# The last pair's fold and the mixing's first sums: one step or three

## The chip, the cores and the metric

The kernel runs on one core of a Trainium2 chip. The metric is the device time of one execution in microseconds (us). The kernel before has a median of 1599.43 us over three runs (1600.13, 1599.43 and 1596.14). One more execution was recorded by the hardware profiler; that one is what the profile below shows.

## The reference

For each of 8 batches and 8 heads (sequence length 576, head size 64), attention keeps only scores within `tau` of the row's maximum. The heads' outputs are joined to rows of 512, and those go through a Fourier mixing, a layer norm and a two-layer channel network:

```python
scores = np.matmul(q, k.transpose(0, 1, 3, 2)) / np.sqrt(64)
thresh = np.max(scores, axis=-1, keepdims=True) - tau
attn = softmax(np.where(scores >= thresh, scores, -1e9))
x = np.matmul(attn, v).transpose(0, 2, 1, 3).reshape(8, 576, 512)

mixed = np.real(np.fft.fft(np.fft.fft(x, axis=1), axis=2))
u = x + mixed
un = (u - mean(u)) / np.sqrt(var(u) + 1e-6)
out = u + np.maximum(un @ w_ch1, 0.0) @ w_ch2      # 512 -> 2048 -> 512
```

All of it is in 32-bit floats.

## The kernel before, in words

**Tiling.** The sequence of 576 rows is cut into 5 query tiles (4 of 128 rows, one of 64). Two heads are handled as a pair, so that a batch has 4 pairs x 5 tiles = 20 steps. A step `i` belongs to pair `n` and tile `t`; below, m is the step's number inside its batch, m = `i % 20`. Batches 2 to 7 run in the late loop (L1692 and after), 120 steps. Everything of the two stages is interleaved there: while the attention of batch b runs, the rows of earlier batches go through mixing and channel network.

**One step of the late loop.** It is written out by hand, in this order:

1. `scores(i)`: TensorE (PE) makes the scores of both heads (L427; L433 for the short tile).
2. At t = 3 and t = 1 the values' product `pv` (L627) for a finished half of a pair, whose result ScalarE (ACT) copies out (L634, `x_first`).
3. `softmax_first`: VectorE (DVE) makes the negated row maxima `neg` (L506, two instructions), ACT the exponentials `e` (L512) and the thresholds `thr` (L516).
4. At m = 2: the rest of `last_fold`, then `start_batch`, which makes the mixing of the batch before available and plans the channel work.
5. `fill(True)`: filler matmuls of the channel network for PE. DVE and ACT jobs that these bring along are held back until after step 6.
6. `softmax_second`: DVE cuts `e` at the threshold and sums it (L527), adds a small number to the sum `den` (L531) and inverts it (L534). Then the held jobs.
7. One part of the mixing, if one is open. At t = 1 the fold of the previous pair begins.
8. The transposes of the weights of step i-1: a small one `pe` (L578), then two groups `pw` (L596), with a `fill()` between them.
9. `softmax_third`: ACT scales `e` by 1/`den` (L540). At t = 3 `prep_pair` transposes the next pair's keys and queries on DVE (L398, L399, L401).
10. `factors()` of a row group whose statistics are ready, then a last `fill()`, which also takes one part of the mixing.
11. DMA issues on SyncE (SP): `load_v` at t = 2, `load_pair` at t = 4.

**What orders the work.** Each engine takes its instructions in the order in which this loop issues them. PE's filler is metered by a budget: `per_slot` is the work still to do, less a reserve `keep`, divided by the number of fills in a batch. A unit of 2048 stands for one block of four 128x512 matmuls. With `keep` the loop leaves 3 x 7 such blocks over for later. `ps.tile(..., tag="mm", bufs=4)` are four banks of PSUM that `pw`, `pv`, `py`, `po` and others share: a new use of a bank waits until the old content was read.

**The fold of a batch's last pair** (`fold_rows`, L660 to L698) is on DVE; for the other pairs it is on GpSimd (POOL). It takes the pair's output `x` and makes two `half` rows (L678, sum and difference with the mirrored row), four pieces of `f` from them (L683), and two small ones for the edges (L690, L694). At m = 1 both `half` instructions and all four pieces are issued, at m = 2 the small ones.

**The mixing** (`mixing`, L719 and after) is a generator. It first forms sums and differences over channel chunks, `fold_chunks` (L709 sums, L710 differences, 128x608 each), then the even and odd parts of `f` (L735, L731 twice, L731 for two more, L740; 128x304 each). After that the matmuls `py` (L750) read `f`, ACT copies them to `y_e` and `y_o` (L755, L760), `pa` (L767, L771) follow, and POOL adds the residual (L792). In the kernel before all of L709, L710, L735, L731 and L740 are issued at m = 2, and the first `py` at m = 3 just ahead of that step's `pe` and `pw`.

**Rows** (`Rows`, L824 and after) holds a group of 512 output rows. `load` turns them around through PSUM (`pn`, L836), ACT copies them to `u` (L842), DVE takes mean and variance (L844, L845). `factors` makes the inverse deviation: ACT takes the square root (L852), loads the table of the exponential again (L855), and DVE inverts the root (L856). `add` (L863) uses the result.

There are six places where a batch ends inside the late loop (m = 1 to 3 of steps 40, 60, 80, 100, 120 and 140 and after) and one after the loop, at the end of batch 7. I call the six *transitions* and the last one the *tail*.

Of the kernel before, what the change touches and what calls it, by code (L numbers as in the profile page):

```python
# [47 lines left out]
def kernel(  # L48
# [12 lines left out]
    nc = tc.nc  # L61
    B, H, S, D = q.shape
    DM = H * D
# [5 lines left out]
    NJ = HID // 128  # L69
# [7 lines left out]
    BT = 512  # L77
# [13 lines left out]
    FW = 304  # L91
# [297 lines left out]
            )  # L389

    def prep_pair(n):

        q_raw, k_raw = loaded.pop(n)
        kT = sb.tile([128, D + S], FP32, tag="kT", name="kT")
        nc.vector.transpose(kT[:, D : D + S], k_raw[:, :])  # L398
        nc.vector.transpose(kT[64:128, 0:D], k_raw[64:128, 512:S])  # L399
        qT = sb.tile([128, S], FP32, tag="qT", bufs=1, name="qT")  # L400
        nc.vector.transpose(qT[:, :], q_raw[:, :])  # L401
        heads[n] = (qT, kT, v_in[n % 2])
        if n + 1 < B * NPAIR and not late:
            load_pair(n + 1)
# [255 lines left out]
    def fold_rows(n):  # L660
        b, p = n // NPAIR, PAIRS[n % NPAIR]
        if late and n % NPAIR == 0:
            assert not mixes
            x = sb.tile([128, S], FP32, tag=f"x{p}", bufs=1, name=f"x{p}")
            nc.gpsimd.tensor_copy(x[:, :], xs[b][p][:, :])
            xs[b][p] = x
            swap_rows(n)
            yield
        x = xs[b][p]

        half = sb.tile([128, 2, HALF], FP32, tag="half", bufs=1, name="half")
        up, down = x[:, 1:HALF], _reversed(x[:, HALF + 1 : S])
        mid = S // 4

        last = n % NPAIR == NPAIR - 1
        eng = nc.vector if last else nc.gpsimd
        for c, op in enumerate((ALU.add, ALU.subtract)):
            eng.tensor_tensor(out=half[:, c, 1:HALF], in0=up, in1=down, op=op)  # L678
        yield
        for c, c0, op in (  # L680
            (0, 0, ALU.add), (0, 161, ALU.subtract), (1, FW, ALU.subtract), (1, FW + 161, ALU.add)
        ):
            eng.tensor_tensor(  # L683
                out=f[:, p, c0 : c0 + mid - 1], in0=half[:, c, 1:mid],
                in1=_reversed(half[:, c, mid + 1 : HALF]), op=op,
            )
            if late and last and c0 > 0 and c0 != FW:
                yield

        eng.tensor_tensor(  # L690
            out=f[:, p, mid - 1 : mid + 1], in0=_stepped(x, mid, -mid, 2),
            in1=_stepped(x, 3 * mid, -mid, 2), op=ALU.add,
        )
        eng.tensor_tensor(  # L694
            out=_stepped(f[:, p, :], 160, FW, 2), in0=_stepped(x, 0, mid, 2),
            in1=_stepped(x, HALF, mid, 2), op=ALU.subtract,
        )
        yield  # L698


        if n % NPAIR == 1 and b != 1:
            fold_halves(b)
# [3 lines left out]
        fold_chunks(nc.gpsimd, b, 1)  # L706

    def fold_chunks(eng, b, c):
        eng.tensor_tensor(out=sums[b][:, c, :], in0=f[:, c, :], in1=f[:, c + 2, :], op=ALU.add)  # L709
        eng.tensor_tensor(  # L710
            out=f[:, c + 2, :], in0=f[:, c, :], in1=f[:, c + 2, :], op=ALU.subtract
        )
# [6 lines left out]
    def mixing(b):  # L719
# [3 lines left out]


        E, O = slice(0, FW), slice(FW, 2 * FW)
        fold_chunks(nc.vector, b, 0)
        yield 0
        s01 = sums.pop(b)

# [94 lines left out]
    class Rows:  # L824
# [26 lines left out]
        def factors(self):  # L851
            nc.scalar.activation(  # L852
                out=self.rstd[:, :], in_=self.mv[:, :, 1], func=ACT.Sqrt, bias=eps[:, :], scale=1.0
            )
            nc.scalar.activation(out=warm[:, :], in_=eps[:, :], func=ACT.Exp)  # L855
            nc.vector.reciprocal(self.rstd[:, :], self.rstd[:, :])  # L856

        def add(self, t, cols, product):

            u = self.us[t][:, cols]  # L860
            if len(product.shape) == 3:
                u = u.rearrange("p (j n) -> p j n", j=2)
            nc.vector.scalar_tensor_tensor(  # L863
                out=u, in0=product, scalar=self.rstd[:, t : t + 1], in1=u,
                op0=ALU.mult, op1=ALU.add,
            )
# [574 lines left out]
    late = []  # L1441
    ended = []


    mixes = []
# [3 lines left out]
    per_batch = NPAIR * NT  # L1449
# [1 line left out]
    holding = []  # L1451
    held = []

    def fill(hold=False):
        nonlocal budget, spent
        holding[:] = [True] if hold else []
        budget += per_slot
        if mixes and not ended and not hold:
            mix(1)
        while work and spent < budget and work[0][0] < mixed:  # L1460
            done = next(work[0][1], None)
            if done is None:
                work.pop(0)
            else:
                spent += done
        holding.clear()
        if mixes and ended:
            mix(1)
# [123 lines left out]
    def start_batch(b):  # L1592

        nonlocal groups, todo, per_slot, budget
        mixes.append(mixing(b))
        todo += MIX
        while groups < NG and BT * (groups + 1) <= (b + 1) * S:
            rows = Rows(groups)
            work.append((b, channels(rows) if groups == 0 else two_level(groups, rows), rows))
            todo += cost(groups)  # L1600
            groups += 1

        keep = 4 * BT * NJ * DM // 128 if b == 0 else 3 * 7 * 2048
        per_slot = (todo - spent - keep) / (3 * per_batch)
        budget = spent

    def mix(count):
        nonlocal spent, mixed
        for _ in range(count):
            done = next(mixes[0], None)  # L1610
            if done is None:
                mixes.pop(0)
                mixed += 1
                break
            spent += done
# [72 lines left out]
        fold_more()  # L1688

    late.append(True)  # L1690

    for i in range(2 * per_batch, total):  # L1692


        n, t = divmod(i, NT)
# [11 lines left out]
            softmax_first(i)  # L1707
        next(values, None)
        if i % per_batch == 2:
            for _ in last_fold:  # L1710
                pass
            start_batch(i // per_batch - 1)
        fill(True)
        if i < total:
            softmax_second(i)
        while held:
            held.pop(0)()
        if mixes:
            mix(1)
        if t == 1:  # L1720
            if n % NPAIR:
                folds.append(fold_rows(n - 1))
            else:
                last_fold = fold_rows(n - 1)
                next(last_fold)
# [8 lines left out]
        if i < total:  # L1734
            softmax_third(i)
            if t == 1:
                prep_ends(n)
            if t == 2 and n + 1 < B * NPAIR:
                scale_q(n + 1)
            if t == 3 and n + 1 < B * NPAIR:  # L1740
                prep_pair(n + 1)
        if wanted:
            wanted.pop().factors()
        if i % per_batch == 1:
            next(last_fold)
        fill()
        if t == 2 and n + 1 < B * NPAIR:
            load_v(n + 1)
        if t == 4 and n + 2 < B * NPAIR:
# [21 lines left out]
    last_fold = fold_rows(B * NPAIR - 1)  # L1771
# [66 lines left out]
```

## Time and profile before

| what | value |
|---|---|
| median of three runs | 1599.43 us |
| the profiled execution, whole | 1599.32 us |
| its span, first to last instruction | 1596.8 us |
| PE busy | 1538.9 us (96% of the span) |
| DVE / ACT / POOL busy | 1097.3 / 908.5 / 805.1 us |
| mean granted PE clock | 0.989 of full speed |
| `half` L678 on DVE, shortest / median | 439 / 1372 ns |
| 1/rstd L856 on DVE, median | 177 ns, 9 times |

The profiled execution is 0.1 us under the median, and 2.5 us of its time lie outside the span. In the answers of the trace a line gives the start in us, the time in us, the engine, the line of the kernel, the operation, what it writes and reads (out<-in), the shape, and how many instructions stand in the group. In square brackets stands how long the engine stood idle before it, and what ended that. In tables by window, the share of time busy of each engine is followed by the number of its instructions, and after them come the granted PE clock (1.00 is full), the share of the DMA engines' time and their rate.

### The profile page before, as it was taken

To read this page: it belongs to the slowest core of one execution; us is meant where nothing else is said; L and a number is where in the kernel's file an instruction comes from. 1 tells how busy PE (TensorE), PEld (TensorE's weight loads), DVE (VectorE), ACT (ScalarE), POOL (GpSimd) and SP (SyncE) were. 2 spreads that over 40 slices of the span, in tenths; PEclk is the share of its full clock that TensorE was granted. 3 is DMA by queue.
4 is the path that set the end of the run, shared out by engine and by line. 5 is a ranking of instruction groups with operands and counts; after the bars stand their busy time and mean duration, and the time that the engine had idled before them with its cause. 6 is when DMAs were issued, how large, how long until landed. Compare 5 with 4: busy or idle time off the path is not lost.

```text
span 1596.8 us, 27063 instructions
## 1 busy us (share of the span) xinstructions
PE 1538.9 (96%) x9786; PEld 1191.1 (75%) x9786; DVE 1097.3 (69%) x2148; ACT 908.5 (57%) x1873; POOL 805.1 (50%) x1009
## 2 busy tenths in 40 slices
PE   8999989999999999989999999999999999999999
PEld 4555445555788877877787878877787778889999
DVE  6997886855869566775668567756577666655546
ACT  5775665554665566656666576656666666222231
POOL 6784665034445552546254633545264625546735
PEclk9999999999999999999999999999999999999999
DMA  6423221556956254634455345635464434546655
GB/s 156 134 58 115 75 76 36 161 154 201 301 171 205 77 158 127 201 112 142 133 159 160 119 129 151 184 101 155 128 181 127 135 124 150 200 150 226 242 192 186
DMA packets 248906, 239.30 MB, mean 150 GB/s; under 512 B 197027, under 2 KB 218533, under 8 KB 228678
## 3 DMA queue, kind: packets, MB, share of 16 engines
q1 hardware_dynamic: 246262, 237.28, 49.9%
q8 instruction: 78, 1.28, 0.3%
q10 hardware_dynamic: 2512, 0.30, 0.2%
q14 instruction: 54, 0.44, 0.1%
HBM read 205.93 MB, written 31.46 MB: 149 GB/s over the span
## 4 chain that ended last, share of the span: by engine, by line
PE 77%; DVE 14%; ACT 4%; issue 2%; POOL 2%; DMA 2%; SPq 0%; DVEq 0%; ACTq 0%; POOLq 0%
PE ph L1178 24%; PE po L1365 17%; PE pv L627 8%; PE sc L427 7%; PE pw L596 6%; PE po L901 4%; PE ph L877 2%; DVE e L467 2%; PE py L750 2%; PE sc L433 1%; PE pa L767 1%; DVE neg L451 1%; PE pe L578 1%; PE pa L771 1%; PE po L1344 1%
## 5 line engine op out<-in xcount | busy, mean ns | idle before, releaser
L512 ACT ACTIVATE e<-sc,neg 128x576 f32<-128x576 f32 x216 | 158.6, 734 | 139.2 <-DVE neg L506 138.8
L506 DVE TENSOR_REDUCE neg<-sc 128x1 f32<-128x576 f32 x216 | 154.0, 750 | 110.7 <-PE sc L427 103.1
L1365 PE MATMUL po<-w,w_all 128*128 128x128 f32 x1728 | 220.9, 278 | 0.8 <-ACT ends L584 0.8
L1365 PEld LDWEIGHTS po<-w,w_all 128*128 128x128 f32 x1728 | 206.9, 193 | 10.2 <-issue 5.5
L1115 DVE TENSOR_TENSOR hs<-ph,hs 128x512 f32<-128x512 f32 (+1 forms) x128 | 105.2, 822 | 157.8 <-PE ph L1178 101.7
L1124 POOL TENSOR_TENSOR w<-hs 128x512 f32<-128x512 f32 x32 | 42.1, 1318 | 317.4 <-ACT hs L1120 243.6
L596 PE MATMUL pw<-ident,e 128*128 128x128 f32 x1152 | 172.9, 277 | 17.9 <-ACT x_first L634 9.0
L1178 PE MATMUL ph<-u_t,w 128*128 128x256 f32 x768 | 180.5, 381 | 0.7 <-DMA w<-f 0.4
L527 DVE SCALAR_TENSOR_TENSOR e<-sc,thr,e 128x576 f32<-128x576 f32 x216 | 168.2, 812 | 17.7 <-ACT thr L516 17.5
L427 PE MATMUL sc<-kT,qT 64*128 64x288 f32 x1024 | 171.3, 434 | 9.1 <-DVE e L467 8.0
L598 ACT COPY e_t<-pw 128x512 f32<-128x512 f32 x256 | 148.7, 594 | 46.7 <-PE pw L596 45.5
L540 ACT ACTIVATE e<-e,den 128x576 f32<-128x576 f32 x216 | 157.6, 775 | 17.3 <-DVE den L534 16.4
L596 PEld LDWEIGHTS pw<-ident,e 128*128 128x128 f32 x1152 | 136.7, 142 | 36.3 <-ACT x_first L634 10.1
L1178 PEld LDWEIGHTS ph<-u_t,w 128*128 128x128 f32 x768 | 141.2, 190 | 23.5 <-issue 4.4
L1178 PE MATMUL ph<-w_all,w 128*128 128x256 f32 x672 | 157.1, 382 | 1.1 <-DVE w_all L1100 1.0
L427 PEld LDWEIGHTS sc<-kT,qT 64*128 64x128 f32 x1024 | 94.5, 188 | 64.2 <-issue 33.9
L1178 PEld LDWEIGHTS ph<-w_all,w 128*128 128x128 f32 x672 | 123.4, 190 | 23.9 <-issue 4.9
L1120 ACT ACTIVATE hs<-hs 128x512 f32<-128x512 f32 (+1 forms) x96 | 74.1, 771 | 114.1 <-DVE hs L1115 113.0
L1230 POOL TENSOR_TENSOR w_all<-w_all 128x128 f32<-128x128 f32 (+2 forms) x160 | 117.8, 753 | 29.9 <-DVE w_all L1385 22.4
L1365 PE MATMUL po<-w,hs 128*128 128x128 f32 x912 | 120.2, 279 | 0.0
L1365 PEld LDWEIGHTS po<-w,hs 128*128 128x128 f32 x912 | 110.5, 193 | 9.4 <-issue 7.2
L792 POOL TENSOR_TENSOR u_t<-x,tmp 128x289 f32<-128x289 f32 (+1 forms) x45 | 34.5, 766 | 104.8 <-DVE tmp L787 104.8
(225 smaller groups left out, 2996.7 us busy)
## 6 DMA issues: line engine op xcount, KB each, us to landing
w<-f SPq DMA_DIRECT2D x150, 1024.0 KB, 4.9
hs<-in_moe_w_ch_dram SPq DMA_DIRECT2D x23, 512.0 KB, 4.4
q_in<-in_q_dram SPq DMA_DIRECT2D x128, 72.0 KB, 3.3
out_dram<-u SPq DMA_DIRECT2D x36, 256.0 KB, 2.3
k_in<-in_k_dram SPq DMA_DIRECT2D x124, 72.0 KB, 3.1
v_in<-in_v_dram SPq DMA_DIRECT2D x64, 128.0 KB, 5.0
f<-w SPq DMA_DIRECT2D x14, 512.0 KB, 4.0
f<-w SPq DMA_DIRECT2D x7, 1024.0 KB, 4.8
```

The source lines that it names most:

```text
L427: nc.tensor.matmul(sc[j][:, c, 0:HALF], qT[hp, 128 * t : 128 * t + 128], kT[hp, k0 + HALF * c : k0 + HALF * (c + 1)], start=True, stop=True,)
L506: nc.vector.tensor_reduce(out=neg[:, j : j + 1], in_=sc[j][:, :, 0:HALF], axis=AXIS_XY, op=ALU.max, negate=True,)
L512: nc.scalar.activation(out=ej, in_=sc[j][:, :, 0:HALF], func=ACT.Exp, bias=neg[:, j : j + 1], scale=1.0)
L527: nc.vector.scalar_tensor_tensor(out=ej, in0=sc[j][:, :, 0:HALF], scalar=thr[:, j : j + 1], in1=ej, op0=ALU.is_ge, op1=ALU.mult, accum_out ...
L540: nc.scalar.activation(out=e[:, S * j : S * (j + 1)], in_=e[:, S * j : S * (j + 1)], func=ACT.Copy, scale=den[:, j : j + 1],)
L596: nc.tensor.transpose(pw[:, c, :], e[:, c0 : c0 + 128], ident[:, :])
L598: nc.scalar.copy(e_t[:, 4 * j : 4 * j + 4, qs], pw[:, :, :])
L627: nc.tensor.matmul(pv[64 * j : 64 * j + 64, 0:m], vt[:, 2 * c + j, :], e_t[:, 4 * j + c, 0:m] if c < 4 else ends[:, 0, 0:m], start=(c == 0 ...
L1115: nc.vector.tensor_tensor(out=to, in0=bank, in1=to if other is None else other, op=ALU.add)
L1178: nc.tensor.matmul(bank[:, 256 * q : 256 * q + 256].rearrange("p (two n) -> p two n", two=2), left[:, 256 * c + 128 * q : 256 * c + 128 * ...
L1230: return lambda: eng.tensor_tensor(out=to, in0=to, in1=other, op=ALU.add)
L1365: nc.tensor.matmul(to, lefts[m][j][:, s], right_[:, 128 * s : 128 * (s + 1)], start=jn in (0, 4) and s == 0, stop=s == 3, skip_group_check ...
```

## The change

- **The fold of the last pair**, for batches that end inside the loop (`apart`): the second `half` instruction goes to the last part of m = 1, after the step's second filler. Two pieces of `f` are issued in m = 2 before `softmax_second`, the other two and the small ones in m = 2 after it, in the place of that step's mixing part.
- **The mixing's first sums**: `chunks_in_parts` yields between L709 and L710. The last filler of m = 2 takes no part of the mixing. A new `mix(1)` stands in m = 3 ahead of `softmax_second`.
- **The pair's preparation**: `pair_in_parts` makes the transposed keys at t = 3 and the transposed queries at t = 4, in every pair of the late loop.
- **The inverse deviation** is made in the first `add` instead of in `factors`.
- **The reserve** `keep` of the late loop is 24 blocks instead of 21.

The number of instructions of each kind is the same.

```diff
@@ -389,14 +389,16 @@
             )
 
     def prep_pair(n):
+        for _ in pair_in_parts(n):
+            pass
+
+    def pair_in_parts(n):
 
         q_raw, k_raw = loaded.pop(n)
         kT = sb.tile([128, D + S], FP32, tag="kT", name="kT")
         nc.vector.transpose(kT[:, D : D + S], k_raw[:, :])
         nc.vector.transpose(kT[64:128, 0:D], k_raw[64:128, 512:S])
+        yield
         qT = sb.tile([128, S], FP32, tag="qT", bufs=1, name="qT")
         nc.vector.transpose(qT[:, :], q_raw[:, :])
         heads[n] = (qT, kT, v_in[n % 2])
@@ -674,8 +676,11 @@
 
         last = n % NPAIR == NPAIR - 1
         eng = nc.vector if last else nc.gpsimd
+        apart = late and last and b < B - 1
         for c, op in enumerate((ALU.add, ALU.subtract)):
             eng.tensor_tensor(out=half[:, c, 1:HALF], in0=up, in1=down, op=op)
+            if apart and c == 0:
+                yield
         yield
         for c, c0, op in (
             (0, 0, ALU.add), (0, 161, ALU.subtract), (1, FW, ALU.subtract), (1, FW + 161, ALU.add)
@@ -684,7 +689,7 @@
                 out=f[:, p, c0 : c0 + mid - 1], in0=half[:, c, 1:mid],
                 in1=_reversed(half[:, c, mid + 1 : HALF]), op=op,
             )
-            if late and last and c0 > 0 and c0 != FW:
+            if late and last and (c0 == 161 or c0 > FW and not apart):
                 yield
 
         eng.tensor_tensor(
@@ -706,7 +711,12 @@
         fold_chunks(nc.gpsimd, b, 1)
 
     def fold_chunks(eng, b, c):
+        for _ in chunks_in_parts(eng, b, c):
+            pass
+
+    def chunks_in_parts(eng, b, c):
         eng.tensor_tensor(out=sums[b][:, c, :], in0=f[:, c, :], in1=f[:, c + 2, :], op=ALU.add)
+        yield 0
         eng.tensor_tensor(
             out=f[:, c + 2, :], in0=f[:, c, :], in1=f[:, c + 2, :], op=ALU.subtract
         )
@@ -723,7 +733,11 @@
 
 
         E, O = slice(0, FW), slice(FW, 2 * FW)
-        fold_chunks(nc.vector, b, 0)
+        apart = late and b < B - 1
+        if apart:
+            yield from chunks_in_parts(nc.vector, b, 0)
+        else:
+            fold_chunks(nc.vector, b, 0)
         yield 0
         s01 = sums.pop(b)
 
@@ -853,10 +867,13 @@
                 out=self.rstd[:, :], in_=self.mv[:, :, 1], func=ACT.Sqrt, bias=eps[:, :], scale=1.0
             )
             nc.scalar.activation(out=warm[:, :], in_=eps[:, :], func=ACT.Exp)
-            nc.vector.reciprocal(self.rstd[:, :], self.rstd[:, :])
+            self.inverted = False
 
         def add(self, t, cols, product):
 
+            if not self.inverted:
+                nc.vector.reciprocal(self.rstd[:, :], self.rstd[:, :])
+                self.inverted = True
             u = self.us[t][:, cols]
             if len(product.shape) == 3:
                 u = u.rearrange("p (j n) -> p j n", j=2)
@@ -1451,11 +1468,11 @@
     holding = []
     held = []
 
-    def fill(hold=False):
+    def fill(hold=False, apart=False):
         nonlocal budget, spent
         holding[:] = [True] if hold else []
         budget += per_slot
-        if mixes and not ended and not hold:
+        if mixes and not ended and not hold and not apart:
             mix(1)
         while work and spent < budget and work[0][0] < mixed:
             done = next(work[0][1], None)
@@ -1600,7 +1617,7 @@
             todo += cost(groups)
             groups += 1
 
-        keep = 4 * BT * NJ * DM // 128 if b == 0 else 3 * 7 * 2048
+        keep = 4 * BT * NJ * DM // 128 if b == 0 else (24 if late else 21) * 2048
         per_slot = (todo - spent - keep) / (3 * per_batch)
         budget = spent
 
@@ -1688,6 +1705,7 @@
         fold_more()
 
     late.append(True)
+    coming_pair = []
 
     for i in range(2 * per_batch, total):
 
@@ -1707,16 +1725,23 @@
             softmax_first(i)
         next(values, None)
         if i % per_batch == 2:
-            for _ in last_fold:
-                pass
+            next(last_fold)
             start_batch(i // per_batch - 1)
+        if i % per_batch == 3:
+            mix(1)
         fill(True)
         if i < total:
             softmax_second(i)
         while held:
             held.pop(0)()
-        if mixes:
+        if i % per_batch == 2:
+            for _ in last_fold:
+                pass
+        elif mixes:
             mix(1)
+        if t == 4 and coming_pair:
+            for _ in coming_pair.pop():
+                pass
         if t == 1:
             if n % NPAIR:
                 folds.append(fold_rows(n - 1))
@@ -1738,12 +1763,11 @@
             if t == 2 and n + 1 < B * NPAIR:
                 scale_q(n + 1)
             if t == 3 and n + 1 < B * NPAIR:
-                prep_pair(n + 1)
+                coming_pair.append(pair_in_parts(n + 1))
+                next(coming_pair[0])
         if wanted:
             wanted.pop().factors()
-        if i % per_batch == 1:
-            next(last_fold)
-        fill()
+        fill(apart=i % per_batch == 2)
         if t == 2 and n + 1 < B * NPAIR:
             load_v(n + 1)
         if t == 4 and n + 2 < B * NPAIR:
```

## The prediction

> **What bounds the kernel now.** I read the page first: PE is busy nearly always, so only its pauses can be won.
>
> ```profile
> PE 1538.9 (96%) x9786; PEld 1191.1 (75%) x9786; DVE 1097.3 (69%) x2148; ACT 908.5 (57%) x1873; POOL 805.1 (50%) x1009
> ...
> PE 77%; DVE 14%; ACT 4%; issue 2%; POOL 2%; DMA 2%; SPq 0%; DVEq 0%; ACTq 0%; POOLq 0%
> ```
>
> The second line is the chain that ended last. Next I read PE's timeline around each transition. In the late loop PE pauses almost only there. The one at step 122:
>
> ```profile
> 1030.35 0.66 PE L596 MATMUL pw<-ident,e 128*128 128x128 f32 x4 [0.50 <-ACT ends L584]
> 1039.50 0.30 PE L578 MATMUL pe<-ident,e 128*128 128x128 f32 x1 [0.57 <-DVE w_all L1385]
> 1041.99 0.85 PE L596 MATMUL pw<-ident,e 128*128 128x128 f32 x4 [2.19 <-ACT x_first L634]
> ```
>
> The same three pauses stand at 102 and 142; at 62 they are 0.90 + 2.19, at 82 0.75 + 0.84 + 2.62 + 0.25, at 42 only 0.17. Sum of the five: 3.09 + 4.46 + 3.24 + 3.26 + 3.25 = 17.3 us. The releaser is named, its reason isn't: DVE's timeline shows it (start, us; leaving out the read-outs).
>
> ```profile
> 1032.39 1.17 DVE L531 TENSOR_SCALAR den<-den 128x2 f32<-128x2 f32 x1
> ...
> 1034.05 0.78 DVE L709 TENSOR_TENSOR sums<-f 128x608 f32<-128x608 f32 x1
> 1034.87 0.79 DVE L710 TENSOR_TENSOR f<-f 128x608 f32<-128x608 f32 x1
> 1035.70 0.48 DVE L735 TENSOR_TENSOR f<-sums 128x304 f32<-128x304 f32 x1
> ...
> 1037.53 0.97 DVE L731 SCALAR_TENSOR_TENSOR f<-f,factors 128x304 f32<-128x304 f32 x2
> ...
> 1039.27 1.42 DVE L506 TENSOR_REDUCE neg<-sc 128x1 f32<-128x576 f32 x2
> ```
>
> DVE is never free here, and `neg` of m = 3 stands last in its queue. ACT's `exp` (L512) waits for it, the copy `x_first` stands behind `exp`, and PE's `pw` wants the PSUM bank of that copy. At 102 the scores started at 860.66 and `neg` at 867.19: a lag of 6.5 us. I call that difference L3 (L2, L4 for the other steps).
>
> After the pause PE runs at half clock for a while (windows of 1 us: PE busy, then the clock in the eighth column):
>
> ```profile
> 1041.00:1042.00 1.00, 0.01 (x1) 0.02 (x1) 1.00 (x1) 1.00 (x4) 0.57 (x1) 1.00 0.93 377
> 1042.00:1043.00 1.00, 1.00 (x6) 0.92 (x7) 1.00 (x4) 0.65 (x4) 0.00 (x0) 0.66 0.30 115
> 1043.00:1044.00 1.00, 1.00 (x7) 1.00 (x7) 0.93 (x5) 0.73 (x2) 0.00 (x0) 0.50 0.00 0
> ```
>
> The four windows from 1042 lose 0.34 + 0.50 + 0.50 + 0.36 = 1.70 us. It is there after four of the five pauses (not at 102): 6.7 us. In the tail PE waits 2.82 us, then the clock is low from 1383 to 1391; the busy part of that costs about 2.8 us:
>
> ```profile
> 1384.59 0.80 PE L750 MATMUL py<-dim_c,f 128*128 128x128 f32 x2 [2.82 <-DVE f L731]
> ```
>
> Everything that the change can reach is thus 17.3 + 6.7 + 5.6 = 29.6 us.
>
> **What the Trainium skill says.** "SBUF — State Buffer", section "Who interferes with whom": a DVE instruction with two SBUF inputs contends with a GpSimd instruction that reads SBUF, and the one that comes second is blocked whole. The trace agrees: `half` L678 takes 0.44 us at its shortest and 1.37 in the median, and at 102 the two took 2.8 us while POOL ran L1136. "TensorE: Matmul & The Clock Gate", section "What's actually happening": after an idle window of about 3.4 us the clock falls to half, and comes back after about as long. The trace has the half clock, for about 3.3 us, after shorter pauses (0.57 + 2.19 with 0.30 of work between), and once no drop after the same ones; so the same pause need not cost the same. "ScalarE: Activation LUTs", section "What ACT_TABLE_LOAD costs": 1283 ns of loading; the trace has 1.28 us at L852 and L855 each.
>
> **The change part by part.** Durations are the trace's. First the balance as it was, at 102: L3 = L2 + DVE's work in m = 2 - PE's work in m = 2. Before, L2 was 3.4 (852.24 to 855.68), DVE needed 11.5 (to 867.19), PE's step took 8.4: 3.4 + 11.5 - 8.4 = 6.5, as seen.
>
> *m = 1.* Before, DVE's time between its `neg` of m = 1 and m = 2 was 12.1 us, in it 3.08 of waiting for ACT's `u` ahead of L844 and 1.0 for four pieces of `f` (4 x 0.25). The pieces go to m = 2. With the reserve of 24, `per_slot` is a little smaller; in the built order L844 thereby moves to the end of m = 1 and its wait off the front of `softmax_second`. What stays (`neg` 1.42, `e` 1.6, the two sums 0.35, two `half` 0.8 to 2.8, three or four 128x512 additions 2.4, L844 and L845 0.86, some contention) is about 9.5 us; PE has 9.9. So L2 comes down to its floor of 1.2 to 1.8; I take 1.8.
>
> *m = 2.* DVE in the built order: `neg` 1.42, pieces 0.5, `e` 1.6, sum and inverse 0.35, pieces 0.5, small ones 0.3, L709 0.8, two additions 1.24, L856 0.17, one L863 0.4. That is 7.3 us; PE has 7.5. L3 = 1.8 + 7.3 - 7.5 = 1.6, with one or two blocked instructions (each 1 us, as L531 above with 1.17 for 0.17) up to 3.4. I take 3.0. L856 adds no wait in this place: the root is ready as long as its two table loads (2 x 1.28 + 0.5 = 3.1 us on ACT), now in the end of m = 2, are through; from nothing to 1 us. In `factors` it waited 2.4 us in two of nine cases, mostly hidden; I count no gain for it.
>
> *m = 3.* `pw` wants the bank of `x_first`, ready at L3 + 2.65 (`neg` 0.71, two `exp`, the copy), at 5.4 us after the scores: a pause of 0.25 at L3 = 3. The first `py` wants the third and fourth L731. DVE ahead of their end: `neg` 1.42, L710 0.8, one addition 0.6, `e` 1.6, sum and inverse 0.35, L863 0.4, L735 and L731 0.45 + 0.45, half of the pair 0.45: L3 + 6.5. PE comes to it after scores 1.17, `pv` 2.31, two blocks 1.8, `pe` and `pw` 0.55, two blocks 1.8, `pw` 0.44: 8.1, with issue gaps about 8.3. The pause of the step in total is L3 - 1.8 = 1.2 us (nothing at L3 = 1.6; 2.5 with another blocked instruction). The stall thus moves in part from `pw` to `py`, and is shorter. DVE has 9.5 in this step as PE has, so L4 is 1.9, and m = 4 with its little work on DVE catches up; I count 0.3 there for ACT's `y` copies. Left over: 1.5 us per transition.
>
> *Queries at t = 4*, in 23 pairs. L401 costs 0.78 us on DVE either way. It lies after `e` now, about 4 us after that step's scores began; the next pair's scores come about 7 us after them. Some 2.5 us are spare at an ordinary pair, 0.4 after m = 4 of a transition. Cost nothing; if the cover is gone, the delay for each pair. `load_pair` on SP's queue waits for L401 and `load_v` stands behind it: up to a step later, while each pair is loaded two pairs ahead, 7 us or more before use against 3.3 us to land. Nothing.
>
> *The reserve.* Three blocks, 3 x 0.895 = 2.7 us of PE, are done later, not more. No gain in itself.
>
> *The tail.* The fold keeps its old order there, but with 3 more blocks left, and statistics one fill later, `half` runs ahead of L844, where DVE sat idle 4.92 us (1365.36). By the same count the last L731 ends about 18.9 us after `pv`, `py` comes at 19.2 (before 22.6): the 2.8 us go, and with them the low clock, 2.8. POOL is busy there, one L731 pair took 2.99 for 0.9, so from nothing to 5.6; I take 5.6.
>
> *Sum.* Pauses 17.3 - 5 x 1.5 = 9.8; low clock: [...] I let one of the four stay, 5.0; tail 5.6: 20.4 us. From the profiled 1599.3: 1579. The median is 0.1 above it, so the same number stands for it. Own range 1573 to 1588: all blocked instructions absent, or L3 at 3.4 and half of the tail lost.
>
> **The rivals.** *A, the stall only changes its name.* With POOL's 1.3 us instructions in the way twice or three times a transition, L3 is 4.5 and `py` waits 2.7; with `x_first` before it this is the old pause of 2.8 and the clock falls as before. The gain is then 0 to 2 us of pauses a transition, no clock, and little of the tail: 1588 to 1599, 1593 as its middle. For it: L531 and L690 are blocked each time in the trace of before; against it: DVE has some 4 us less ahead of `neg`.
>
> *B, slower: the queries become the bound.* PE waits ahead of L427 of a new pair for L401, because DVE is still busy at t = 4. The turn is at a wait of 20.4 / 23 = 0.9 us a pair, which eats all that is gained; at 1.2 us it is 1579 + 27.6 = 1607. L401 would have to come 2.5 + 1.2 = 3.7 us later than I count at each ordinary pair. For it: it is moved in every pair, and spare time after transitions is 0.4 us only. Against: DVE is 69% busy, and t = 4 has half of the softmax's work.
>
> *C, all of it goes*: L3 at 1.6 everywhere and no wait in the tail: 1599.3 - 29.6 = 1570.
>
> *D, no effect*: the pauses have another cause than DVE's order; 1599. The gapless DVE timeline speaks against it.
>
> **How the numbers follow.** Forecast 0.62, A 0.20, B 0.06, C 0.10, D 0.02. About 0.3% (4.8 us) is what a measurement of this kernel can tell from no change, so faster is under 1594.6: forecast, C and 0.12 of A: 0.84; within: 0.08 of A and D: 0.10; slower: B, 0.06. The range leaves out B, D, the upper 0.07 of A and the lower 0.05 of C: 1571 to 1595.
>
> **What would show it.** Right: no pause over 2 us at `pw` behind L634 at steps 62 to 142, L3 under 3.5, the mean clock above 0.989, no 2.82 before `py` in the tail, PE's busy time down by 5 to 8 us (that is the clock). Wrong: a pause of 2 us or more before the first `py`; pauses of PE before L427 behind L401; ACT's `exp` behind the table loads of L852 at m = 3.

## The result

The changed kernel takes 1604.27 us (median of 8 runs, 1602.78 to 1607.11), the kernel before in the same series 1599.88 us (8 runs, 1596.14 to 1602.57). The ratio is 1.0024, with a 95% interval from 1.0014 to 1.0035: a little slower, by some 4 us, where 20 us less were forecast. The profiled execution of the changed kernel took 1602.78 us, with a span of 1600.4 us against 1596.8.

The page first:

```profile
PE 1539.2 (96%) x9786; PEld 1190.7 (74%) x9786; DVE 1107.7 (69%) x2148; ACT 906.1 (57%) x1873; POOL 816.6 (51%) x1009
...
PE 73%; DVE 16%; ACT 5%; issue 2%; POOL 1%; DMA 1%; SPq 0%; DVEq 0%; ACTq 0%; POOLq 0%
```

PE is busy for 0.3 us more, though the change adds no work. DVE and POOL are busy for 10.4 and 11.5 us more with the same instructions, and the chain of waits runs through DVE and ACT more than before. Then PE's timeline from step 123 on:

```profile
1044.65 1.29 PE L764 MATMUL py<-dim_c,f 128*128 128x65 f32 x6 [1.87 <-DVE f L749]
...
1051.10 0.65 PE L764 MATMUL py<-dim_c,f 128*48 128x65 f32 x6 [0.52 <-DVE w_all L1402]
1052.02 0.66 PE L598 MATMUL pw<-ident,e 128*128 128x128 f32 x4 [0.28 <-ACT y_o L769]
...
1060.29 0.51 PE L781 MATMUL pa<-seq_odd,y_o 128*128 128x144 f32 x2 [0.63 <-ACT y_o L769]
...
1087.42 1.97 PE L1195 MATMUL ph<-t_room,w 128*128 128x256 f32 x8 [0.40 <-DVE hs L1132]
...
1139.55 1.24 PE L429 MATMUL sc<-kT,qT 64*128 64x288 f32 x8 [0.60 <-DVE qT L403]
```

Before, there were two pauses behind each other, 0.57 and 2.19 us, both at m = 3. Now m = 3 has one of 1.87 us, and then come small ones where there had been none: at m = 4 (step 124), m = 5, m = 8 and, at m = 15 (step 135), ahead of the scores. In the list of waits for the whole kernel (us in total, times, longest) three kinds stand out:

```profile
PE py L764 <- DVE f L749: 6.4, 4, 1.9
...
PE pw L598 <- ACT x_first L636: 4.6, 2, 2.9
PE sc L429 <- DVE qT L403: 3.1, 5, 0.8
```

**A ledger of PE's lost time.** Many waits are too short for these views, so I made a sum from the trace and call it the ledger. For each matmul I took the time from its start to the next matmul's start, less what this form of matmul usually needs for it (the lower third of all its cases in both kernels). What is over is lost: waits, half clock, and a part that every step has. Added up by stretch, with the kernel before taken off, in us:

| stretch | all | of it low clock |
|---|---|---|
| m = 2 and 3, six transitions | -12.0 | -2.8 |
| m = 4 to 8, six transitions | +12.0 | +1.1 |
| m = 9 to the next m = 1 | +5.4 | 0 |
| tail | -1.4 | -1.7 |
| start to step 41 | -0.4 | 0 |

The sum is +3.6 us, the difference of the two spans. The old pauses were indeed shortened. Everything won there was paid back within the next five steps, and 5.4 us more were lost where the transitions are long over, 3.3 us of it in the first batch after step 49, with this pause in step 58:

```profile
470.65 1.16 PE L1382 MATMUL po<-w,w_all 128*128 128x128 f32 x8 [1.79 <-DVE w_all L1176]
```

DVE's timeline at step 121 to 123 (`neg` of m = 2 at 1028.26, of m = 3 at 1038.46):

```profile
1027.43 0.69 DVE L858 BATCH_NORM_STATS2 stats<-u 128x6 f32<-128x512 f32 x1 [3.20 <-ACT u L856]
...
1028.26 1.39 DVE L508 TENSOR_REDUCE neg<-sc 128x1 f32<-128x576 f32 x2
1029.56 1.15 DVE L688 TENSOR_TENSOR f<-half 128x143 f32<-128x143 f32 x2
...
1033.89 1.77 DVE L1176 TENSOR_TENSOR w_all<-hs 128x512 f32<-128x512 f32 x1
1035.79 1.55 DVE L1176 TENSOR_TENSOR w_all<-w_all,hs 128x512 f32<-128x512 f32 x1
...
1038.46 1.42 DVE L508 TENSOR_REDUCE neg<-sc 128x1 f32<-128x576 f32 x2
```

Two things are to be seen. At m = 1 DVE stands idle for 3.20 us, while pieces that were done there before are now waiting for m = 2. And in m = 2 the two additions of L1176, for which I had taken 0.62 us each, take 1.77 and 1.55 while POOL runs adds of its own. From `neg` to `neg` that is 10.2 us, not 7.3. The lag at m = 3 (from the start of the scores to `neg`) is 4.3 us at three transitions, 4.6 and 6.0 at the other two (before 6.5 to 8.5).

### The profile page after: what moved, and what is told of

Same layout as the page of the kernel before. It is cut to its first block, busy times and chain, and to the rows that moved or that the text cites. A ratio compares the mean times of both kernels' runs of the same rounds, so it can differ in the third digit from the quotient of the medians.

```text
span 1600.4 us, 27094 instructions
## 1 busy us (share of the span) xinstructions
PE 1539.2 (96%) x9786; PEld 1190.7 (74%) x9786; DVE 1107.7 (69%) x2148; ACT 906.1 (57%) x1873; POOL 816.6 (51%) x1009
## 4 chain that ended last, share of the span: by engine, by line
PE 73%; DVE 16%; ACT 5%; issue 2%; POOL 1%; DMA 1%; SPq 0%; DVEq 0%; ACTq 0%; POOLq 0%
PE ph L1195 23%; PE po L1382 16%; PE pv L629 8%; PE sc L429 7%; PE pw L598 5%; PE po L918 4%; PE ph L894 2%; DVE w_all L1176 2%; DVE e L469 2%; DVE e L529 1%; PE sc L435 1%; PE py L764 1%; DVE neg L508 1%; PE pa L781 1%; DVE neg L453 1%
## 5 line engine op out<-in xcount | busy, mean ns | idle before, releaser
L1382 PEld LDWEIGHTS po<-w,w_all 128*128 128x128 f32 x1728 | 207.5, 194 | 16.1 <-issue 9.7
L542 ACT ACTIVATE e<-e,den 128x576 f32<-128x576 f32 x216 | 157.2, 773 | 12.9 <-DVE den L536 12.8
L1247 POOL TENSOR_TENSOR w_all<-w_all 128x128 f32<-128x128 f32 (+2 forms) x160 | 118.4, 757 | 19.9 <-DVE w_all L1402 13.9
L681 POOL TENSOR_TENSOR half<-x 128x287 f32<-128x287 f32 x48 | 38.7, 828 | 119.7 <-DMA x<-swap 68.2
```

The costliest lines, as they stand in the source:

```text
L542: nc.scalar.activation(out=e[:, S * j : S * (j + 1)], in_=e[:, S * j : S * (j + 1)], func=ACT.Copy, scale=den[:, j : j + 1],)
L1247: return lambda: eng.tensor_tensor(out=to, in0=to, in1=other, op=ALU.add)
L1382: nc.tensor.matmul(to, lefts[m][j][:, s], right_[:, 128 * s : 128 * (s + 1)], start=jn in (0, 4) and s == 0, stop=s == 3, skip_group_check ...
```

## The experiments

Each kernel below the first row was measured beside the kernel before, whose median in these series was 1600.2 to 1601.0 us. In the names, q stands for the queries, r for the inverse deviation, s for the sums, k for the reserve and f for the fold; what is undone is as it was before the change. Ledger columns are PE's lost time against the kernel before, in us, as above.

| kernel | median, us | ratio (95%) | m 2-3 | m 4-8 | m 9-1 | tail |
|---|---|---|---|---|---|---|
| changed | 1604.27 | 1.0024 (1.0014 to 1.0035) | -12.0 | +12.0 | +5.4 | -1.4 |
| q_undone | 1603.68 | 1.0016 (1.0010 to 1.0023) | -12.9 | +12.3 | +5.4 | -1.5 |
| r_undone | 1605.26 | 1.0030 (1.0019 to 1.0040) | -12.2 | +12.9 | +5.4 | -1.3 |
| s_undone | 1622.17 | 1.0129 (1.0116 to 1.0143) | +5.5 | +12.1 | +5.2 | -1.4 |
| k_undone2 | 1606.01 | 1.0033 (1.0020 to 1.0046) | -3.3 | +11.0 | -1.3 | +0.2 |
| f_undone | 1598.46 | 0.9983 (0.9977 to 0.9990) | -17.9 | +12.1 | +5.4 | -0.3 |
| k_alone | 1608.28 | 1.0044 (1.0031 to 1.0057) | +0.8 | +2.7 | +5.6 | -1.3 |
| py_late | 1596.42 | 0.9968 (0.9956 to 0.9979) | -12.9 | +11.2 | -1.1 | -2.3 |
| py_late1 | 1611.63 | 1.0062 (1.0046 to 1.0078) | -1.0 | +15.1 | -1.1 | -0.7 |
| copy_first | 1597.86 | 0.9985 (0.9973 to 0.9998) | -2.8 | +0.1 | -0.2 | -2.4 |
| py_late_copy | 1596.39 | 0.9969 (0.9959 to 0.9979) | -18.9 | +16.9 | -0.9 | -2.2 |
| catch_up | 1606.61 | 1.0035 (1.0023 to 1.0047) | -11.4 | +17.0 | +5.7 | -2.4 |
| fold_old_reserve_21 | 1597.54 | 0.9979 (0.9972 to 0.9986) | -10.2 | +10.2 | -0.5 | -1.3 |
| fold_old_reserve_23 | 1602.85 | 1.0012 (1.0006 to 1.0019) | -13.1 | +5.5 | +10.5 | +0.2 |
| fold_old_reserve_25 | 1597.71 | 0.9983 (0.9976 to 0.9989) | -20.2 | +13.9 | +5.2 | -0.7 |
| y_on_dve | 1601.78 | 1.0008 (1.0002 to 1.0015) | -16.8 | +16.1 | +5.5 | -3.1 |
| small_before | 1577.65 | 0.9855 (0.9839 to 0.9872) | -21.2 | +0.1 | +0.1 | +0.8 |
| small_after | 1586.98 | 0.9916 (0.9901 to 0.9931) | -24.4 | +8.9 | +5.5 | -2.8 |

The ledger is of one profiled execution each. Its start, up to step 41, differs by up to 4 us between executions (low clock) and is left out. In the other columns one low stretch more or less is 1.7 us, so that differences of this size say little.

Seven of the runs (k_undone2, the three with py_late in their names, and the three with fold_old_reserve) carry a second edit, shown at k_undone2. It keeps POOL from beginning the fold of the next pair while the mixing is open. No run has this edit alone, so that what it does by itself is not shown.

### One part undone

**The queries.**

```diff
-                coming_pair.append(pair_in_parts(n + 1))
-                next(coming_pair[0])
+                prep_pair(n + 1)
```

> The changed kernel with the pair's queries transposed at t = 3 again, all else changed. Theory 1 (the wait for L403 is a cost of its own): the five pauses of 0.53 to 0.81 us ahead of the scores go, 3.1 us: about 1601. Theory 2 (PE would have waited for something else there): under 1 us of difference, 1603 to 1605. Rival (L401 was in the way in m = 3 of a transition): slower than the changed kernel by 1 to 4 us.

1603.68 us, 0.6 less than the changed kernel and inside the run-to-run spread: theory 2. The waits behind L403 are real, but with the queries back at t = 3 PE loses the same in the same stretches: `po` now waits 1.54 us at step 79 and 1.52 us at step 119.

**The inverse deviation.**

```diff
-            self.inverted = False
+            nc.vector.reciprocal(self.rstd[:, :], self.rstd[:, :])
...
-            if not self.inverted:
-                nc.vector.reciprocal(self.rstd[:, :], self.rstd[:, :])
-                self.inverted = True
```

> The changed kernel with the inverse deviation made in factors again. DVE then waits for ACT's root behind the end of m = 2, ahead of neg of m = 3. If that wait is hidden as the prediction says: 1604, within 1.5 us of the changed kernel. If it is not: a lag at m = 3 up by 1 to 2 us at five transitions, 1609 to 1614.

1605.26 us: no difference that these runs can tell. The wait was hidden.

**The sums.**

```diff
-            yield from chunks_in_parts(nc.vector, b, 0)
+            fold_chunks(nc.vector, b, 0)
...
-        if i % per_batch == 3:
-            mix(1)
...
-        fill(apart=i % per_batch == 2)
+        fill()
```

> The changed kernel with the mixing's first sums and differences in one part at m = 2 again, no mixing part ahead of the softmax at m = 3, and the last filler of m = 2 taking one; the first py comes one part earlier than in the changed kernel. Theory 1 (what is paid back in m = 4 to 8, 12.0 us in the sum of six transitions, comes from the mixing being two parts late): about half of it comes back, and m = 3 loses 0 to 1 us each: 1599 to 1602. Theory 2 (spreading the sums is the useful part): lag at m = 3 up to 5 to 6 us, old pauses and clock drops again, 1607 to 1612.

1622.17 us, 18 us slower than the changed kernel. Theory 1 falls: the first `py` is one part earlier, and m = 4 to 8 lose 12.1 us as before. Theory 2 holds in kind and was too small: the lag at m = 3 is 6.1 to 8.5 us, and m = 2 and 3 lose 17.5 us more than in the changed kernel. But this edit does two things. It also brings the first `py` to the place that it has in py_late1 below, and there `py` waits 1.92 us for `x_first` at three transitions, as it does in py_late1. How much of the 18 us is the sums' own stays open.

**The reserve.**

```diff
-        keep = 4 * BT * NJ * DM // 128 if b == 0 else (24 if late else 21) * 2048
+        keep = 4 * BT * NJ * DM // 128 if b == 0 else 21 * 2048
...
     def fold_more():
-        if folds and next(folds[0], True):
+        if folds and not (late and mixes) and next(folds[0], True):
```

The second edit goes with the first because of a condition in `fold_rows`: the fold of a batch's first pair may not begin while a mixing is open.

> The changed kernel with the reserve of 21 blocks (a fold of the next pair is not begun while the mixing is open). Theory 1 (the reserve makes the 5.4 us lost between the transitions, since the kernel before with a late py, which has the old reserve, lost nothing there): 1597 to 1600. Theory 2 (it moves L844's wait off m = 1 and saves at the transitions): 1606 to 1610.

1606.01 us, 1.7 more than the changed kernel, which is not clear of noise. Both theories are half right: the 5.4 us between the transitions go (-1.3), and m = 2 and 3 lose 8.7 us more. The lag at m = 3 is about the same, 4.7 us; PE waits 4.01 us at three transitions for L749, ahead of the first `py`.

> The kernel before with the reserve of 24 blocks and nothing else. Theory 1: 3 to 6 us slower than before, with the loss between the transitions and most of it after the first of them: 1603 to 1606. Theory 2 (the reserve helps the transitions): 1594 to 1598, with a lower lag at m = 3.

The edit is the reserve of 24 in the kernel before. 1608.28 us: slower than theory 1 had it. The loss between the transitions is there with 5.6 us and nothing else of the change, and 2.7 us at m = 4 to 8 come with it. All nine kernels with 24 lose 5.2 to 5.7 us between the transitions, the seven others with 21 nothing there (+0.1 to -1.3). That the reserve costs this is shown. From this kernel's list of waits:

```profile
PE po L1365 <- DVE w_all L1379: 3.2, 2, 1.6
PE ph L1178 <- DVE hs L1115: 2.4, 6, 0.4
PE po L1365 <- DVE w_all L1159: 1.8, 1, 1.8
```

The first and the third line lie between the transitions, at steps 79, 119 and 58. The second is another cost of the reserve: five of its six waits stand at m = 8. The ledger has 3.2 us there, and the same 3.2 us in the changed kernel.

**The fold.**

```diff
-        apart = late and last and b < B - 1
+        apart = False
...
         if i % per_batch == 2:
-            next(last_fold)
+            for _ in last_fold:
+                pass
             start_batch(i // per_batch - 1)
...
             wanted.pop().factors()
+        if i % per_batch == 1:
+            next(last_fold)
         fill(apart=i % per_batch == 2)
```

> The changed kernel with the whole fold at m = 1 and its small pieces at m = 2 ahead of the softmax as before; the mixing has the times of the changed kernel. If the fold's split helps at m = 2 and 3 (1.0 us of pieces and the small ones moved): the lag at m = 2 up, at m = 3 the same or less, within 2 us: 1603 to 1606. If the split is what delays f for py: py waits less and it is faster, 1598 to 1602. If it shortens the lag at m = 3 by more than that: 1608 to 1612.

1598.46 us: 5.8 us faster than the changed kernel, and faster than the kernel before. None of the three reasons was quite it: `py` doesn't wait less (2.21 us at step 123), but the lag at m = 3 falls from 4.3 to 6.0 us to 3.3 to 3.8. DVE's timeline there:

```profile
1019.87 2.04 DVE L688 TENSOR_TENSOR f<-half 128x143 f32<-128x143 f32 x4
1023.16 0.69 DVE L858 BATCH_NORM_STATS2 stats<-u 128x6 f32<-128x512 f32 x1 [1.26 <-ACT u L856]
...
1032.44 0.18 DVE L875 RECIPROCAL rstd<-rstd 128x4 f32<-128x4 f32 x1 [1.44 <-ACT rstd L866]
```

The four pieces lie in the time in which DVE waits for ACT's `u` anyway: the wait of 3.20 us is 1.26. In m = 2 DVE is now so early that it waits 1.44 us for the root. The fold's split had moved work from a hole into the full step.

### The first py

**Two parts later.** In the kernel before:

```diff
         nc.vector.tensor_tensor(out=f[:, 0, O], in0=s01[:, 0, O], in1=s01[:, 1, O], op=ALU.subtract)
         yield 0
+        if late and b < B - 1:
+            yield 0
+            yield 0
```

and the same edit of `fold_more` as above.

> The kernel before with two empty parts ahead of the first py, so that py, pa and all after them come two parts later, as in the changed kernel; fold, sums and all else stay (a fold of the next pair is not begun while the mixing is open). Theory 1 (a late mixing costs 2 us a transition by itself): 8 to 12 us slower than before, 1608 to 1612. Theory 2 (m = 4 to 8 pay for DVE's work moved there): within 2 us of before.

1596.42 us: both theories fall, and this is one of the two fastest kernels here that compute everything. DVE's order is the old one and its lag at m = 3 the old 6.5 us, yet m = 2 and 3 lose 12.9 us less, as much as in the changed kernel. PE's timeline at step 123:

```profile
1034.23 1.24 PE L427 MATMUL sc<-kT,qT 64*128 64x288 f32 x8
1040.90 0.66 PE L596 MATMUL pw<-ident,e 128*128 128x128 f32 x4 [1.03 <-DVE w_all L1388]
```

Only at step 83 a long pause stays (3.07 us). So the old pause needs two things: a late `neg`, and a bank that is met too early. By the order of issue and the releasers in the traces, the four banks go round. In the kernel before, m = 3 takes them for `pv`, `po`, `py` and `pe`; the next, `pw`, meets that of `pv`, which ACT reads behind the exponentials. Without `py` in the row, `pw` takes the fourth bank, and its pause is 1.03 us.

**One part later.** The edit is one `yield 0` instead of two.

> The kernel before with one empty part ahead of the first py instead of two, so that py comes between the two groups of pw at m = 3. Bank theory (in the kernel before the first py takes the one of the four banks after which pw meets the bank of x_first; with py behind the first pw, that pw meets an older bank): the pauses at m = 2 and 3 go nearly as with two parts (-9 to -13 us), and the mixing is late by one part only, which gives back 3 to 8 in place of 11: 1591 to 1597. Theory 2 (the delay of py helps because f is ready later): py now waits for f in its place, 1598 to 1602.

1611.63 us: the bank theory named the bank rightly and the time wrongly. Now it is `py` that waits for the copy out of the bank of `pv`:

```profile
1050.16 0.66 PE L596 MATMUL pw<-ident,e 128*128 128x128 f32 x4 [1.04 <-DVE w_all L1387]
1052.74 0.94 PE L752 MATMUL py<-dim_c,f 128*128 128x65 f32 x6 [1.92 <-ACT x_first L634]
...
1093.24 0.65 PE L627 MATMUL pv<-e_t,v_rev 128*64 128x256 f32 x2 [1.66 <-DVE hs L1117]
```

The last line is at m = 8. Of the 15.1 us that m = 4 to 8 lose here, 11.4 lie at that step, where `pv` meets a bank whose reader is late. So this loss too depends on which tile comes next, and not on the delay as such.

**The bank freed earlier.**

```diff
         next(values, None)
+        if i % per_batch == 3:
+            next(values, None)
         if i < total:
             softmax_first(i)
```

> The kernel before with ACT's copy of x_first at m = 3 issued ahead of the exponentials of that step instead of behind them; nothing of DVE's order changes. Bank theory (what holds pw is the bank of pv, which is read only behind exp, which waits for neg): the five pauses of 2.19 to 2.87 us go with their clock drops, 11 + 5 us, of which the next tiles of the ring take back half: 1585 to 1594. Theory of the prediction (DVE's lag as such holds PE, through exp and the weights): the pause comes back one tile later, 1597 to 1601.

1597.86 us, a gain of some 2.4 us by the ratio (0.3 to 4.3) and not of 6 to 15: the prediction's theory is right here. The pause comes back one tile later, for the next bank that ACT reads behind the exponentials:

```profile
1042.16 0.71 PE L750 MATMUL py<-dim_s,f 128*128 128x128 f32 x4 [1.99 <-ACT y_e L760]
```

> The same edit on the kernel before with py two parts late. Bank theory: there the bank of x_first is not met in time anyway, pauses of 1.03 us at w_all stay: within 3 us of that kernel, 1593 to 1597. If the long pause of 3.07 us at step 83 goes with it: 1591 to 1594.

1596.39 us, the same as without the copy. m = 2 and 3 lose 6 us less, m = 4 to 8 5.7 us more.

### What m = 4 to 8 pay

**The mixing brought forward again.**

```diff
-        if i % per_batch == 3:
+        if 3 <= i % per_batch <= 5:
             mix(1)
```

> The changed kernel with one more part of the mixing in m = 4 and one in m = 5, so that it is as early as before from m = 5 on. Lateness theory (the 12 us of m = 4 to 8 are paid because the mixing is two parts late): 4 to 8 us faster, 1596 to 1600. Rival (they are paid because DVE's work moved into m = 3 leaves neg of m = 4 late and ACT's copies behind it): denser parts wait more, 1604 to 1610.

1606.61 us: my lateness theory, as I had put it, falls. The stretch loses 17.0 us in place of 12.0, and the waits are again for the copies of `py`:

```profile
1056.72 0.65 PE L598 MATMUL pw<-ident,e 128*128 128x128 f32 x4 [0.40 <-ACT y_o L769]
1064.23 0.51 PE L781 MATMUL pa<-seq_odd,y_o 128*128 128x144 f32 x2 [0.93 <-ACT y_o L769]
```

**The copies of py on another engine** (in the kernel with the old fold).

```diff
-                nc.scalar.copy(
+                copy = nc.vector.tensor_copy if apart else nc.scalar.copy
+                copy(
                     y[0:n, u, 0:256].rearrange("p (g hi lo) -> p lo hi g", hi=2, lo=2),
...
-                    nc.scalar.copy(y[0:n, u, 256:257], py[0:n, 0:1])
+                    copy(y[0:n, u, 256:257], py[0:n, 0:1])
```

> The changed kernel with the fold as before and the copies of py to y_e and y_o on DVE in place of ACT. If m = 4 to 8 pay because ACT's y copies stand behind the exponentials that wait for a late neg: about half of the 12 us there comes back, 1591 to 1595. If the mixing's parts wait for banks and f in any case, or DVE's copies stand behind as much work: no gain or slower, 1598 to 1604.

1601.78 us, 3.3 slower than f_undone, and 4 us more lost in the stretch. Taking these copies from ACT's queue doesn't take the loss away: `pa` now waits for DVE's copies, 6.2 us in four places.

**Reserves of 21, 23 and 25 with the old fold.** The edits are those of f_undone, the edit of `fold_more`, and the number.

> The changed kernel with the fold as before and the reserve of 21 blocks (a fold of the next pair is not begun while the mixing is open). If the reserve's two effects are independent (it costs 6.7 us between the transitions and 1.7 to 2.8 in m = 4 to 8, whatever the fold does), and the fold alone was what made m = 2 full: 1590 to 1594. If the transitions' gain needs the filler order that the reserve of 24 brings (L844 and its wait at the end of m = 1): m = 2 and 3 lose 8 us or more, 1598 to 1602.

> The same with 23 blocks. If the reserve acts by its size (the filler left over): half a microsecond from the run with 24, 1597 to 1600. If it acts by where the fillers fall against the steps: a different set of pauses between the transitions, several us to either side, 1592 to 1606.

> The same with 25 blocks. By size: 1597 to 1600. By place: several us to either side, and the pause of 1.8 us in step 58 gone or elsewhere.

1597.54, 1602.85 and 1597.71 us, and 1598.46 with 24 (f_undone, without the edit of `fold_more`; the run with 25 has the edit and similar losses). It is place and not size: one block fewer costs 4 us, three fewer gain nothing that is clear. With 21 the gain between the transitions is had, and m = 2 and 3 lose 7.7 us of theirs. With 23, m = 4 to 8 lose only 5.5 us and the rest 10.5. The pause in step 58 stays with 25.

**The cut.** How much was DVE's in the first place? In both kernels the fold of the last pair, the sums and the even and odd parts of `f` are cut to 8 or 16 columns. The rest of their work is left out, so the output is not the reference's (here the sums; the others likewise):

```diff
-        eng.tensor_tensor(out=sums[b][:, c, :], in0=f[:, c, :], in1=f[:, c + 2, :], op=ALU.add)
+        W = 16 if eng is nc.vector and late and b < B - 1 else 2 * FW
+        eng.tensor_tensor(out=sums[b][:, c, 0:W], in0=f[:, c, 0:W], in1=f[:, c + 2, 0:W], op=ALU.add)
```

> The kernel before with the last pair's fold and the mixing's first sums cut to 8 or 16 columns each (same number, order and places; six transitions; the remaining columns of f are left as they were, so that the output isn't the reference's). It measures how much of the pauses is DVE's. If DVE's lag is the whole cause: the lag at m = 3 under 3 us, the pauses and clock drops of m = 2 and 3 gone, 1575 to 1580. If PE waits there in any case (banks, ACT): 1588 or more.

1577.65 us, 23.2 less than before. The lag at m = 3 is still 3.6 to 4.8 us, but of the pauses over 0.3 us one is left at m = 3 (step 83), and at m = 2 two, of 0.74 and 0.45 us:

```profile
686.68 0.33 PE L578 MATMUL pe<-ident,e 128*128 128x128 f32 x1 [1.33 <-ACT x_first L634]
...
1018.15 0.65 PE L596 MATMUL pw<-ident,e 128*128 128x128 f32 x4 [0.45 <-ACT ends L584]
```

> The changed kernel with the same cut. If m = 4 to 8 lose because DVE is late there: the 12 us fall to under 4, and the time to 1577 to 1583. If they lose because the mixing begins two parts later and the reserve shifts the fillers: 8 to 12 us stay there and 5 between the transitions, 1588 to 1594.

1586.98 us: with the same cut the changed order is 9.3 us slower than the old one. Of the 12.0 us of m = 4 to 8, 8.9 stay without DVE's load; the 5.5 us between the transitions stay too.

```profile
1034.22 0.91 PE L768 MATMUL py<-dim_c,f 128*128 128x65 f32 x6 [1.36 <-DVE f L749]
1048.67 0.51 PE L785 MATMUL pa<-seq_odd,y_o 128*128 128x144 f32 x2 [0.63 <-ACT y_o L773]
1075.81 1.97 PE L1199 MATMUL ph<-t_room,w 128*128 128x256 f32 x8 [0.40 <-DVE hs L1136]
1127.94 1.24 PE L429 MATMUL sc<-kT,qT 64*128 64x288 f32 x8 [0.60 <-DVE qT L403]
```

The last three pauses are those of the changed kernel, to 0.01 us. Only the first of these three is the mixing's: `ph` behind `hs` at m = 8 is the reserve's, as in k_alone, and the last one is the queries'. Without the 3.2 us of m = 8, 5.7 of the 8.9 are left.

## Why the prediction was wrong, point by point

**What the change can reach: right.** The pauses and clock drops of m = 2 and 3 were counted as 17.3 + 6.7 = 24.0 us and put down to DVE. Cutting DVE's work away gave 23.2 us.

**m = 1: right in number, wrong in what it overlooked.** The lag at m = 2 came out as 1.8 us at four of five transitions (2.7 at 102). But I counted the pieces of `f` as a gain for m = 1. That step had a wait for ACT, of 3.08 us at 101 before and of 3.20 at 121 after. With the reserve of 24 alone, and nothing moved out of m = 1, the lag at m = 2 is the same 1.8 (k_alone; 2.7 at 102). So the reserve made it, and emptying the step won nothing on top.

**m = 2: the sum was too small.** DVE needed 10.2 us for my 7.3: the two additions 3.3 for 1.24, the pieces ahead of the softmax 1.15 for 0.5, one more addition of 0.6. I had allowed for one or two blocked instructions and took L3 = 3.0; it is 4.3 to 6.0. With the fold back at m = 1 it is 3.3 to 3.8, so the split of the fold cost 5.8 us, and this is shown.

**m = 3: right in kind.** The stall moved to `py`, as foreseen: 1.87 us at three transitions where I had 1.2, and at 102 one of 2.94 us for `x_first`. The clock fell at three transitions (four before), where I had let one stay: 2.8 us were won of the 5.0. In the ledger m = 2 and 3 gave 12.0 us, where the prediction has 17.3 - 5 x 1.2 + 5.0 = 16.3.

**m = 4: here the prediction failed.** "I count 0.3 there for ACT's `y` copies": 1.5 us for the five, where 12.0 us were lost at six, from m = 4 to 8. I followed DVE's queue to the first `py` and not what comes after it. The mixing begins two parts later, so that all its eleven parts meet other fillers, banks and copies. From the list of waits of the changed kernel:

```profile
PE ph L1195 <- DVE hs L1132: 2.4, 6, 0.4
PE pa L781 <- ACT y_o L769: 2.3, 5, 0.6
PE py L764 <- ACT y_o L769: 2.3, 3, 1.1
```

The last two lines are the term that I had at 0.3. With two smaller kinds (`pw` behind `y_o` 0.9, `py` behind `y_e` 0.5) PE waits 6.0 us for ACT's `y` copies, where the kernel before has 1.0 in its whole list. The first line is not the mixing's: the 3.2 us of m = 8 stand in k_alone as well and belong to the reserve. So 8.8 of the 12.0 us are left for the later mixing, and low clock is 1.1 of these.

That the delay is what costs here shows in the table: the three kernels with the first `py` at its old place (k_alone, copy_first, small_before) lose 0.1 to 2.7 us in this stretch, all those with a later one 5.5 to 17.0. The kernel before with the delay and the edit of `fold_more` (py_late) loses 11.2 us in this stretch, 4.1 of it at m = 7, where `ph` waits mostly for POOL. In the changed kernel with DVE's load cut away 5.7 stay. Making up the delay and taking the copies from ACT both leave the loss where it is. Why the copies come too late in the new order isn't settled, and the size changes with the reserve (5.5 us for the whole stretch with 23).

**The reserve: the second failure.** "No gain in itself" was a statement about work, and the time is set by place. The 24 blocks cost 5.4 us between the transitions, against a gain of 1.3 with 21 (k_undone2), so 6.7 us, and 3.2 us at m = 8. They gave 8.7 us to m = 2 and 3 of the changed kernel, by an order of fillers that nobody had sought. For the whole kernel that is 1.7 us in their favour, which is not clear of noise.

**The queries and the inverse deviation: right.** Both cost nothing that can be measured, though the first one shows as five waits of 3.1 us.

**The tail: too much.** The wait for L745 went, and one of 2.46 us for another addition stands in its place. Low clock halved; 1.4 us were won, not 5.6:

```profile
1388.66 0.77 PE L764 MATMUL py<-dim_s,f 128*128 128x128 f32 x4 [2.46 <-DVE w_all L1402]
```

**The sum.** Forecast -20.4, found +3.6 in the ledger; the 24.0 us between them are 10.5 (m = 4 to 8, 12.0 - 1.5; 3.2 of it the reserve's), 5.4 (between the transitions, the reserve's), 4.3 (m = 2 and 3), 4.2 (tail), less 0.4 at the start. Rival A named the mechanism best (lag of 4.5, wait ahead of `py`), and priced only the place where the stall was, not what the delay does later. Rival B's place was right and its price nothing.

## What to carry to other kernels

When a stall sits where one engine is full, first look for the step in which that engine waits, and put work there; moving it out of a step with a hole into a step without one cost 5.8 us here. When a generator's parts are delayed, every later part of it meets other neighbours, so the price is to be sought in the steps after the stall, and a run with the delay and little else measures it. A meter that places fillers is a change of order, whatever its size: it has to be measured alone.

## What the runs showed that I had not expected

Which tile of a ring of four banks is next decides as much as how late its reader is: the first `py` at its old place, one part later and two parts later gave 1600, 1612 and 1596 us (the last two with the edit of `fold_more`). And the low clock doesn't follow the length of a pause: at step 103 of the kernel before 0.56 + 2.19 us brought none, at step 123 0.57 + 2.19 did, and in the changed kernel, a pause of 1.87 us at step 143 was followed by low clock and the same pause at step 123 wasn't. The windows after these two (clock in the eighth column):

```profile
1219.00:1220.00 1.00, 1.00 (x6) 1.00 (x6) 1.00 (x3) 0.33 (x2) 0.00 (x0) 0.50 0.84 352
...
1045.00:1046.00 1.00, 0.99 (x8) 0.85 (x8) 1.00 (x3) 0.63 (x2) 0.00 (x0) 1.00 1.00 426
```

A forecast from single pauses can therefore be off by 1.7 us for each of them, half of a low stretch of 3.4 us.
